# Splitting the late score products of a fused WKV and MoE kernel into high and low parts

## The chip, the cores and the metric

The kernel runs on one core of one Trainium2 chip. The metric is the device time of one execution in microseconds; lower is better. Before the change the median of three runs is 518.88 us (518.77 to 519.77).

## The reference

Two stages follow each other. The first is a linear attention with decay over `(batch 4, heads 8, time 768, head size 48)`:

```python
for t in range(S):
    cur = einsum('bhd,bhe->bhde', u[None] * k_t, v_t)
    y[:, :, t] = einsum('bhd,bhde->bhe', r_t, state + cur)
    state = w[None, :, :, None] * state + einsum('bhd,bhe->bhde', k_t, v_t)
```

The second takes `x`, which is `y` as 3072 tokens of 384 numbers, through two matrices with 2048 hidden columns. The inputs and the output are float32.

```python
h = x @ w_in          # 3072x384 @ 384x2048
g = h * cos(h)
out = g @ w_out       # 2048x384
```

## The kernel before

**Attention.** Time is cut into chunks of 128 steps; there are 24 chunks (`chunk(i, ...)`, batch `i % 4`). Inside a chunk the recurrence is turned into matrix products: the scores `A = k·r` of all pairs of time steps (`mm_a`, line 785), a mask (`mask`, L791) that keeps one triangle and leaves on the diagonal what ScalarE wrote there (`diagonal`, L775), the products of the scores with `v` and of the carried state with `r` (`mm_x` L805, `mm_x2` L818), and the update of the state (`mm_z` L840). Heads lie in pairs: head `2p` in partitions 0 to 47 and head `2p+1` in partitions 64 to 111, so `kT` and `rT` hold 4 pairs of 112 partitions x 128 columns, and a chunk has 4 x 2 score products. They are float32; the trace records each as two weight loads (PEld) and two products (PE), 16 of each for a chunk.

The first 12 chunks (`i < XS`) are transposed on TensorE (L696). The other 12 are called `late`: `k` and `r` come in by a second, staged load into the ring `raw` (L659), VectorE transposes them (L704) into `kT` and `rT`, and GpSimd multiplies them with the decay tables (L709). Then `mm_a` runs, and later `mm_xz` with the other products of the chunk.

**MoE.** The tokens form 8 blocks of three chunks (384 columns). Each matrix is kept as a high and a low float32r part, made while the kernel runs (`conv`), and so are `x` (`xh`, `xl`: rings of 12 chunk slots, `R_x`) and `g` (`gh`, `gl`). A product is the sum of three: high·high, high·low, low·high (`mm_h` L282, `mm_o` L288), each one load of 128x128 weights and one product with 384 columns. One step is one block with one group of 128 hidden columns: 9 products of L282, the chain on ScalarE and VectorE (`qi`, `rest`, `cos`, `gate`, `gh`, `gl`), and 9 products of L288. There are 128 steps. The first four blocks go through the hidden columns in turn in four cuts (steps 0 to 63), the other four one after the other.

**Order.** Every operation is an `op` with an engine, a planner's cost, a due time, what it comes after, and the buffers it holds. A list planner (`Plan.order`) gives each engine its order, once, when the program is built; at run time the engines only wait for data and buffers. Loads are issued from the SP queue; a buffer is free again when all its users have run. `xb` gives chunk `i` the slot `i % 12` of `x`'s ring.

**Clock-keeping.** Where the planner sees TensorE idle at the start, `warm_up(n)` puts in small bfloat16 products (L1050). `before` is true until the first `h` has been put out (`o_first`).

Of the kernel before, what the change touches and what calls it, by code (L numbers as in the profile page):

```python
# [15 lines left out]
ALU = mybir.AluOpType  # L16
# [16 lines left out]
XS = 12  # L33
# [40 lines left out]
class Plan:  # L74
# [9 lines left out]
    def op(self, eng, due, cost, emit, after=(), bufs=(), lat=0.2, line=None, port=False):  # L84

        o = Op(eng, due, cost, lat, emit, after, bufs, self.lines.get(line) if line else None, port)
        if line:
            self.lines[line] = o
        self.ops.append(o)
        return o  # L90
# [126 lines left out]
def kernel(  # L217
# [11 lines left out]
    nc = tc.nc  # L229
    PSUM = bass.MemoryType.PSUM  # L230

    B, H, S, D = r.shape
# [3 lines left out]
    C = 128  # L236
    NP = H // 2
    DP = 64
    KP = DP + D
# [3 lines left out]
    NJ = B * CPB  # L243
    TB = max(BLOCKS) * C
    NBLK = len(BLOCKS)
    FIRST = [sum(BLOCKS[:n]) for n in range(NBLK)]
# [22 lines left out]
    def f32(ap):  # L269
        return ap.bitcast(F32)  # L270


    def mm_h(ph, x_hi, x_lo, f):

        fs = slice(f * P, (f + 1) * P)
        mm = []
        for kk in range(NK):
            mm.append((w_in_hi[:, kk, fs], x_hi[:, :, kk, :]))
            mm.append((w_in_hi[:, kk, fs], x_lo[:, :, kk, :]))
            mm.append((w_in_lo[:, kk, fs], x_hi[:, :, kk, :]))  # L280
        for i, (a, b_) in enumerate(mm):
            nc.tensor.matmul(ph, a, b_, start=(i == 0), stop=(i == len(mm) - 1))  # L282
# [19 lines left out]
    with ExitStack() as actx:  # L302
# [19 lines left out]
        xh = att.tile([P, XS, NK, C], F32R, name="xh")  # L322
        xl = att.tile([P, XS, NK, C], F32R, name="xl")
        R_x = [Tile((xh[:, i], xl[:, i])) for i in range(XS)]
# [34 lines left out]
        op = plan.op  # L359
        PE, DVE, ACT, POOL, SP, ACTQ = "PE", "DVE", "ACT", "POOL", "SP", "ACTQ"  # L360
# [22 lines left out]
        def start_dve():  # L383
# [14 lines left out]
            lat=2.2,  # L398
# [41 lines left out]
        def tab_copy():  # L440
# [11 lines left out]
            lat=3.0,  # L452
# [5 lines left out]
        def flag_load():  # L458
            nc.sync.dma_start(b_wr()[0:1, :], w.rearrange("(o h) d -> o (h d)", o=1))
# [144 lines left out]

        last_A = [None]
        last_z = [None] * B

        def flat(buf, p):  # L610
# [8 lines left out]
        def cube(buf):  # L619
            return buf().rearrange("q (p t) -> q p t", p=NP)  # L620

        def chunk(i, due, xbuf):
# [8 lines left out]
            kT, rT = Buf(R_kT), Buf(R_rT)  # L631
            Ap = [Buf(bk) for _ in range(2)]
# [11 lines left out]

            late = i >= XS
            if late:
                rb = Buf(R_f)
                ks, rs = Buf(R_raw), Buf(R_raw)

# [50 lines left out]
            if late:  # L700
# [7 lines left out]
                def decay_s(dst, dec):  # L708
                    return lambda: nc.gpsimd.tensor_tensor(dst()[0:KP], dst()[0:KP], dec[0:KP], op=ALU.mult)  # L709

                t_k = op(DVE, due - 2.9, 0.95, tr_s(kT, ks), [l_ks], [ks, kT])
                e_k = op(POOL, due - 2.8, 1.4, decay_s(kT, decT_k), [t_k], [kT], port=True)
                t_r = op(DVE, due - 2.8, 0.95, tr_s(rT, rs), [l_rs], [rs, rT])
                e_r = op(POOL, due - 2.7, 1.4, decay_s(rT, decT_r), [t_r], [rT], port=True)
            else:
                t_r = op(PE, due - 2.4, 0.49, tr(rTp, rb), [l_r, o_pool], [rb, rTp, rT], lat=0.3)
                e_r = op(
                    DVE,
                    due - 2.2,
                    0.62,  # L720
                    lambda: nc.vector.tensor_tensor(rT()[0:KP], cube(rTp)[0:KP], decT_r[0:KP], op=ALU.mult),  # L721
                    [t_r, o_dtr],
                    [rTp, rT],
                )
# [16 lines left out]
            if first:  # L741
                t_k = op(PE, due - 2.5, 0.49, tr(kTp, kb), [l_k, o_pool], [kb, kTp, kT], lat=0.3)
                e_k = op(
                    DVE,
                    due - 2.3,
                    0.62,
                    lambda: nc.vector.tensor_tensor(kT()[0:KP], cube(kTp)[0:KP], decT_k[0:KP], op=ALU.mult),
                    [t_k, o_dtk],
                    [kTp, kT],
                )  # L750
# [3 lines left out]
            if not first and not late:  # L754
                t_k = op(PE, due - 2.5, 0.49, tr(kTp, kb), [o_kd, o_pool], [kb, kTp, kT], lat=0.3)
                e_k = op(ACT, due - 2.3, 0.5, lambda: nc.scalar.copy(kT()[0:KP], cube(kTp)[0:KP]), [t_k], [kTp, kT])  # L756
# [14 lines left out]
            def diagonal(j):  # L771
                def go():
                    for p in range(NP):
                        h = 2 * p + j
                        nc.scalar.activation(A[j]()[:, p, :], ident, AF.Copy, scale=ab()[:, h : h + 1])  # L775

                return go

            o_d = [op(ACT, due - 1.55 + 0.01 * j, 1.18, diagonal(j), [o_a, o_pool], [ab, A[j]], line="diagonal") for j in range(2)]

            def mm_a():
                for p in range(NP):
                    for j in range(2):
                        ps = slice(j * DP, j * DP + D)
                        nc.tensor.matmul(cube(Ap[j])[:, p, :], kT()[ps, p, :], rT()[ps, p, :], start=True, stop=True)  # L785

            last_A[0] = o_A = op(PE, due - 1.7, 1.25 if late else 1.1, mm_a, [e_k, e_r], [kT, rT, *Ap], lat=0.3)


            def mask(j):  # L790
# [45 lines left out]
            def mm_z():  # L836
                z = zp()[:, 0 : NP * D].rearrange("q (p e) -> q p e", p=NP)
                for h in range(H):
                    p, j = divmod(h, 2)
                    nc.tensor.matmul(z[j * DP : j * DP + D, p, :], kb()[:, h, 0:D], vb()[:, h, 0:D], start=True, stop=True)  # L840
# [10 lines left out]
            if late:  # L851
# [8 lines left out]
                    lat=0.3,  # L860
# [38 lines left out]
        first_h, last_h, need_f = {}, {}, {}  # L899
# [4 lines left out]
        block_of = [n for n in range(NBLK) for _ in range(BLOCKS[n])]  # L904


        xb = [Buf([R_x[i % XS]]) for i in range(NJ)]
        x_ready, x_ready_of = {}, {}
        for i in range(NJ):
            n = block_of[i]  # L910
            t = i - FIRST[n]
            if i < XS:
                due = -6 + 0.9 * i
            else:
                lo, hi = first_h[n - 1], first_h[n] - 1
                if i >= XS:
                    lo = max(lo, last_h[block_of[i - XS]])
                due = lo + (hi - lo) * (t + 1) / BLOCKS[n]
            x_ready.setdefault(n, []).extend(chunk(i, due, xb[i]))
            x_ready_of[i] = x_ready[n][-1]  # L920
# [4 lines left out]
        for i in range(2 * NF):  # L925
            f, part = divmod(i, 2)
            g = max(x for x in group if x <= f)
            if g == 0:
                due = 2 * i - 3.0
            else:  # L930
                lo = need_f[max(x for x in group if x < g)] + 1
                hi = need_f[g] - 1
                n_g = 2 * sum(1 for x in range(NF) if max(y for y in group if y <= x) == g)
                due = lo + (hi - lo) * (i - 2 * g + 1) / n_g
# [3 lines left out]
        lo = need_f[NF - 1] + 10  # L938
# [6 lines left out]
        for s, (n, f, f0, f1) in enumerate(steps):  # L945
# [3 lines left out]
            ph, q, qi, gh, gl = Buf(B_H if n >= GRP else B_HX), Buf(R_f), Buf(R_qi), Buf(R_gh), Buf(R_gl)  # L949
            xs = [xb[FIRST[n] + t] for t in range(nt)]  # L950

            def h(ph=ph, n=n, nt=nt, f=f):
                j = FIRST[n] % XS
                mm_h(ph()[:, 0 : nt * C], xh[:, j : j + nt], xl[:, j : j + nt], f)

            oh = op(PE, s, 9 * (0.0058 + 0.000437 * w_), h, [*x_ready[n], w_ready[2 * f]], [ph, *xs], lat=0.3, line="h")
            if s == 0:
                o_first = oh
            if s in look:
                checks.append(check_range(look[s], s + 4, oh))  # L960
            if s == NS - 14:
# [42 lines left out]
            for t in range(nt):  # L1004
# [6 lines left out]
                if f == f1 - 1:  # L1011
# [16 lines left out]
                    def st(ob=ob, dst=dst, f0=f0, last=last):  # L1028
# [14 lines left out]
                        lat=2.5,  # L1043
# [3 lines left out]
        def warm_up(n):  # L1047
            wp = B_WARM.ap[:, 0:256].rearrange("q (a b) -> q a b", a=2)
            for _ in range(n):
                nc.tensor.matmul(wp, warm, warm[:, None, :].to_broadcast([P, 2, P]), start=True, stop=True)  # L1050

        order = plan.order(PASSES)
        before = True
        with tc.manual_schedule():
            for o in order:
                if before and o.eng == PE:
                    n = int(min(o.gap, 6.0) / 0.2)
                    if n:
                        warm_up(n)
                    before = o is not o_first  # L1060
                o.emit()


# [2 lines left out]
    with tc.If(ok < 1):  # L1066
        with ExitStack() as gctx:
            cp = gctx.enter_context(tc.tile_pool(name="cp", bufs=1))
            for i in range(2 * NF):
                f, part = divmod(i, 2)  # L1070
# [4 lines left out]
                if part == 0:  # L1075
# [4 lines left out]
                    hi, lo, av = w_in_hi[:, :, fs], w_in_lo[:, :, fs], ca.rearrange("p (kk f) -> p kk f", kk=NK)  # L1080
                else:
                    nc.sync.dma_start(raw.rearrange("p f w -> p (f w)"), w_out_w[fs, :])
                    hi, lo, av = w_out_hi[:, f, :], w_out_lo[:, f, :], ca
# [62 lines left out]
            with tc.For_i(0, NT // P, 1) as it:  # L1146
# [10 lines left out]
                for f in range(NF):  # L1157
                    ph = gps.tile([P, P], F32, name="ph")
                    mm_h(ph, x_hi[:, None], x_lo[:, None], f)
                    q = gp.tile([P, P], F32, name="gq")  # L1160
# [41 lines left out]
```

## Time and profile before

| | before |
|---|---|
| median of the runs | 518.88 us |
| the profiled execution | 517.88 us, span 516.2 us |
| mean granted TensorE clock | 0.996 |
| PE busy | 505.9 us (98%) |
| PEld busy (weight loads, beside PE) | 481.3 us (93%) |
| VectorE (DVE) busy | 382.5 us (74%) |
| ScalarE (ACT) busy | 331.7 us (64%) |
| GpSimd (POOL) busy | 177.7 us (34%) |
| score products L785, 384 records | 27.9 us PE, 23.3 us PEld |

A row of a timeline reads: start in us from the span's start, length in us, engine, line, operation, `out<-in`, partitions x columns of weights and of the moving operand, how many records were merged, and in brackets how long the engine was idle before and what ended it. PE is the product, PEld the weight load that belongs to it. A group row gives busy us and mean ns of one.

### The profile page before, as it was taken

How to read it: one execution, taken by the hardware profiler on the slowest of the kernel's cores; microseconds unless marked ns; L12 is line 12 of the kernel's file. 1: busy time of each engine (PE TensorE's matmuls, PEld its weight loads, DVE VectorE, ACT ScalarE, POOL GpSimd, SP SyncE). 2: the span in 40 equal slices, each digit the busy share in tenths (PEclk: the TensorE clock that was granted, in tenths of full speed). 3: DMA queues.
4: the chain of work that ended last, by engine and by line, in shares of the span. 5: the costliest groups of instructions: out<-in, count | busy, mean ns of one | idle time of the engine just before them, and what ended most of it. 6: DMA issues, size and time to landing. Idle time of an engine off the chain costs nothing.

```text
span 516.2 us, 11762 instructions
## 1 busy us (share of the span) xinstructions
PE 505.9 (98%) x4401; PEld 481.3 (93%) x4401; DVE 382.5 (74%) x773; ACT 331.7 (64%) x833; POOL 177.7 (34%) x184
## 2 busy tenths in 40 slices
PE   8999999999999999999999999999999999999994
PEld 6778899999999999999999999999999999999993
DVE  6899889887887876666777777787776768656552
ACT  2979888777776656546667565575665764745452
POOL 6785622364444452242426134214044041300000
PEclk9999999999999999999999999999999999999998
DMA  8996345477775593424675736446265455200001
GB/s 139 182 190 142 76 140 181 141 138 164 159 154 114 138 187 53 65 75 54 161 155 144 161 98 167 111 161 151 83 150 141 144 153 134 67 35 14 1 1 53
DMA packets 114980, 61.61 MB, mean 119 GB/s; under 512 B 78433, under 2 KB 110818, under 8 KB 114914
## 3 DMA queue, kind: packets, MB, share of 16 engines
q1 hardware_dynamic: 109586, 53.50, 42.2%
q0 software_dynamic: 5184, 7.08, 9.8%
q8 instruction: 36, 0.59, 0.5%
q14 instruction: 30, 0.25, 0.2%
q10 hardware_dynamic: 144, 0.20, 0.1%
HBM read 48.96 MB, written 11.80 MB: 118 GB/s over the span
## 4 chain that ended last, share of the span: by engine, by line
PE 95%; DVE 1%; ACT 1%; issue 0%
PE bank L288 40%; PE bank L282 39%; PE bank L785 5%; PE bank L818 4%; PE bank L805 3%; PE bank L696 2%; PE bank L840 2%; PE bank L1050 1%; ACT A L775 0%; DVE A L791 0%; ACT zt L833 0%; DVE zc L887 0%; DVE rT L721 0%; ACT kT L756 0%; DVE w_in_lo L597 0%
## 5 line engine op out<-in xcount | busy, mean ns | idle before, releaser
L288 PE MATMUL bank<-w_out_hi,gh 128*128 128x384 f32 x384 | 132.0, 344 | 0.0
L282 PE MATMUL bank<-xh,w_in_lo 128*128 128x384 f32 x384 | 129.7, 338 | 0.5 <-DVE w_in_lo L597 0.5
L288 PE MATMUL bank<-w_out_hi,gl 128*128 128x384 f32 x384 | 129.7, 338 | 0.0
L288 PE MATMUL bank<-w_out_lo,gh 128*128 128x384 f32 x384 | 129.4, 337 | 0.0
L282 PE MATMUL bank<-xh,w_in_hi 128*128 128x384 f32 x384 | 129.1, 336 | 0.0
L282 PE MATMUL bank<-xl,w_in_hi 128*128 128x384 f32 x384 | 128.7, 335 | 0.0
L296 DVE SCALAR_TENSOR_TENSOR f<-bank,qi 128x384 f32<-128x384 f32 (+1 forms) x132 | 71.2, 542 | 44.3 <-ACT qi L293 43.4
L293 ACT ACTIVATE qi<-bank 128x384 int32<-128x384 f32 (+1 forms) x132 | 62.7, 478 | 55.3 <-PE bank L282 54.6
L989 ACT CAST gh<-f 128x384 fp32r<-128x384 f32 (+1 forms) x132 | 65.7, 500 | 48.6 <-DVE f L986 48.2
L986 DVE TENSOR_TENSOR f<-bank,f 128x384 f32<-128x384 f32 (+1 forms) x132 | 71.1, 541 | 34.8 <-ACT f L299 32.7
L299 ACT ACTIVATE f<-f 128x384 f32<-128x384 f32 (+1 forms) x132 | 67.4, 513 | 44.1 <-DVE f L296 43.3
L992 DVE TENSOR_TENSOR gl<-f,gh 128x384 fp32r<-128x384 f32 (+1 forms) x132 | 79.9, 608 | 19.4 <-ACT gh L989 18.6
L288 PEld LDWEIGHTS bank<-w_out_hi,gh 128*128 128x128 f32 x384 | 72.0, 187 | 3.2 <-issue 1.2
L282 PEld LDWEIGHTS bank<-xh,w_in_lo 128*128 128x128 f32 x384 | 72.1, 188 | 0.8 <-DVE w_in_lo L597 0.8
L282 PEld LDWEIGHTS bank<-xh,w_in_hi 128*128 128x128 f32 x384 | 72.1, 188 | 0.5 <-ACT A L775 0.2
L282 PEld LDWEIGHTS bank<-xl,w_in_hi 128*128 128x128 f32 x384 | 72.1, 188 | 0.0
L288 PEld LDWEIGHTS bank<-w_out_hi,gl 128*128 128x128 f32 x384 | 72.0, 188 | 0.0
L288 PEld LDWEIGHTS bank<-w_out_lo,gh 128*128 128x128 f32 x384 | 72.0, 187 | 0.0
L775 ACT ACTIVATE A<-ident,a 128x128 f32<-128x128 f32 x192 | 59.7, 390 | 6.0 <-DVE a L766 5.9
L709 POOL TENSOR_TENSOR kT<-kT,decT_k 112x512 f32<-112x512 f32 x12 | 15.6, 1301 | 127.6 <-PE bank L282 65.1
L587 POOL TENSOR_TENSOR f<-f,raw 128x384 int32<-128x384 int32 x32 | 36.4, 1137 | 65.9 <-DVE f L576 28.8
L1034 POOL DMA_DIRECT2D out_dram<-f x36 | 32.7, 1012 | 40.1 <-ACT f L1019 31.2
(88 smaller groups left out, 597.1 us busy)
## 6 DMA issues: line engine op xcount, KB each, us to landing
raw<-in_moe_w_in_dram SPq DMA_DIRECT2D x32, 384.0 KB, 3.4
raw<-in_moe_w_out_dram SPq DMA_DIRECT2D x32, 384.0 KB, 3.4
out_dram<-f POOLq DMA_DIRECT2D x36, 192.0 KB, 4.6
k<-in_k_dram SPq DMA_DIRECT2D x24, 192.0 KB, 3.5
v<-in_v_dram SPq DMA_DIRECT2D x24, 192.0 KB, 4.4
raw<-in_k_dram SPq DMA_DIRECT2D x47, 96.0 KB, 2.5
raw<-in_r_dram SPq DMA_DIRECT2D x47, 96.0 KB, 2.5
out_dram<-f SPq DMA_DIRECT2D x23, 192.0 KB, 2.0
```

The lines of the kernel that those rows point to most:

```text
L282: nc.tensor.matmul(ph, a, b_, start=(i == 0), stop=(i == len(mm) - 1))
L288: nc.tensor.matmul(acc, a[:, ts], b_[:, f, :], start=(first and i == 0), stop=(last and i == 2))
L293: nc.scalar.activation(qi, ph, AF.Copy, scale=INV_2PI, bias=0.25)
L296: nc.vector.scalar_tensor_tensor(q, ph, INV_2PI, qi, op0=ALU.mult, op1=ALU.subtract)
L299: nc.scalar.activation(q, q, AF.Sin, scale=TWO_PI, bias=0.5 * math.pi)
L587: lambda: nc.gpsimd.tensor_tensor(ai(), ai(), cn(), op=ALU.add),
L775: nc.scalar.activation(A[j]()[:, p, :], ident, AF.Copy, scale=ab()[:, h : h + 1])
L785: nc.tensor.matmul(cube(Ap[j])[:, p, :], kT()[ps, p, :], rT()[ps, p, :], start=True, stop=True)
L986: nc.vector.tensor_tensor(g()[:, cs], ph()[:, cs], q()[:, cs], op=ALU.mult)
L989: nc.scalar.copy(gh()[:, cs], g()[:, cs])
L992: nc.vector.tensor_tensor(gl()[:, cs], g()[:, cs], f32(gh())[:, cs], op=ALU.subtract)
L1034: nc.gpsimd.dma_start(dst, ob(), accum_op=ALU.add)
```

## The change

The scores of the 12 late chunks are made of three products of high and low parts, as `mm_h` does it. For `kT` and for `rT`, ScalarE copies the float32 values into a float32r part (the high one) and VectorE subtracts this from the values to give the low one. The four parts lie in slots 3, 4 and 5 of `x`'s ring (`xh` for high, `xl` for low), so no new memory is taken; a late chunk's `two` must find these three slots free. The planner's cost of late scores goes from 1.25 to 0.95. The late chunks' own `x` no longer uses slots 3 to 5: block 4 takes slots 0 to 2, block 5 slots 6 to 8, block 6 slots 9 to 11 and block 7 again 0 to 2. And `warm_up` ends at the first score products (`first_A[0]`) in place of the first `h`.

```diff
-        last_A = [None]
+        last_A, first_A = [None], []
...
+                two = [Buf([R_x[n]]) for n in (3, 4, 5)]
...
+            def part(n, low):
+                xs_ = (xl if low else xh)[:, 3:6].rearrange("q i kk t -> q (i kk t)")
+                return xs_[:, n * NP * C : (n + 1) * NP * C].rearrange("q (p t) -> q p t", p=NP)
+
             def mm_a():
+                if late:
+                    mm = ((part(0, 0), part(1, 0)), (part(0, 0), part(1, 1)), (part(0, 1), part(1, 0)))
+                else:
+                    mm = ((kT(), rT()),)
                 for p in range(NP):
-                    for j in range(2):
-                        ps = slice(j * DP, j * DP + D)
-                        nc.tensor.matmul(cube(Ap[j])[:, p, :], kT()[ps, p, :], rT()[ps, p, :], start=True, stop=True)
-
-            last_A[0] = o_A = op(PE, due - 1.7, 1.25 if late else 1.1, mm_a, [e_k, e_r], [kT, rT, *Ap], lat=0.3)
+                    for n, (a, b_) in enumerate(mm):
+                        for j in range(2):
+                            ps = slice(j * DP, j * DP + D)
+                            nc.tensor.matmul(
+                                cube(Ap[j])[:, p, :], a[ps, p, :], b_[ps, p, :], start=(n == 0), stop=(n == len(mm) - 1)
+                            )
+
+            a_in, a_bufs = [e_k, e_r], [kT, rT]
+            if late:
+
+                def split(n, src):
+                    return (
+                        lambda: nc.scalar.copy(part(n, 0)[0:KP], src()[0:KP]),
+                        lambda: nc.vector.tensor_tensor(
+                            part(n, 1)[0:KP], src()[0:KP], f32(part(n, 0))[0:KP], op=ALU.subtract
+                        ),
+                    )
+
+                a_in, a_bufs = [], two
+                for n, (src, made) in enumerate(((kT, e_k), (rT, e_r))):
+                    high, low = split(n, src)
+                    o_h = op(ACT, due - 2.5, 0.5, high, [made], [src, *two])
+                    a_in.append(op(DVE, due - 2.3, 0.62, low, [o_h], [src, *two]))
+            last_A[0] = o_A = op(PE, due - 1.7, 0.95 if late else 1.1, mm_a, a_in, [*a_bufs, *Ap], lat=0.3)
+            first_A.append(o_A)
...
-        xb = [Buf([R_x[i % XS]]) for i in range(NJ)]
+        slot = [i if i < XS else (0, 6, 9)[(i - XS) // 3 % 3] + i % 3 for i in range(NJ)]
+        xb = [Buf([R_x[i]]) for i in slot]
...
-                    lo = max(lo, last_h[block_of[i - XS]])
+                    lo = max(lo, last_h[block_of[max(n for n in range(i) if slot[n] == slot[i])]])
...
-                j = FIRST[n] % XS
+                j = slot[FIRST[n]]
...
-                    before = o is not o_first
+                    before = o is not first_A[0]
```

More of the change, by code (lines that the diff above doesn't have):

```diff
@@ L952, in h @@
             def h(ph=ph, n=n, nt=nt, f=f):
-                j = FIRST[n] % XS
+                j = slot[FIRST[n]]
                 mm_h(ph()[:, 0 : nt * C], xh[:, j : j + nt], xl[:, j : j + nt], f)
             oh = op(PE, s, 9 * (0.0058 + 0.000437 * w_), h, [*x_ready[n], w_ready[2 * f]], [ph, *xs], lat=0.3, line="h")
-            if s == 0:
-                o_first = oh
             if s in look:
```

## The prediction

> **What bounds the kernel now.** I read the page first, then the table of stretches, then the timeline of TensorE around one late chunk, then its weight loads.
>
> ```profile
> span 516.2 us, 11762 instructions
> ...
> PE 95%; DVE 1%; ACT 1%; issue 0%
> ...
> 230.00:280.00 50.00, 50.00 (x423) 48.24 (x422) 36.34 (x70) 32.00 (x83) 19.15 (x19) 1.00 0.56 123
> 280.00:330.00 50.00, 50.00 (x489) 47.36 (x489) 37.93 (x77) 31.53 (x84) 13.72 (x13) 1.00 0.60 140
> ```
>
> The chain that ended last is TensorE for 95% of the span. In the stretches that hold late chunks its busy time is the whole stretch (50.00 of 50 us) at a granted clock of 1.00, while VectorE has some 12 us free in 50 and ScalarE 18. So a microsecond more or less on TensorE there is a microsecond of the result, and work on the other two is covered as long as TensorE does not come to wait for it.
>
> ```profile
> 216.07 0.34 PE L288 MATMUL bank<-w_out_hi,gl 128*128 128x384 f32 x1
> 216.25 0.34 PE L288 MATMUL bank<-w_out_lo,gh 128*128 128x384 f32 x1
> 216.52 1.16 PE L785 MATMUL bank<-rT,kT 48*128 48x128 f32 x16
> 217.61 0.44 PE L288 MATMUL bank<-w_out_hi,gh 128*128 128x384 f32 x1
> 217.89 0.34 PE L288 MATMUL bank<-w_out_hi,gl 128*128 128x384 f32 x1
> ...
> 443.97 1.16 PE L785 MATMUL bank<-rT,kT 48*128 48x128 f32 x16
> ```
>
> These are the first late chunk's scores among MoE products (the last row is the twelfth's). MoE products start 0.18 apart (216.07 to 216.25). From 216.25 to 217.89 there are 1.64 us, of which two MoE products explain 0.35: the scores cost 1.29 us of TensorE in each late chunk. What sets that time is seen in the weight loads.
>
> ```profile
> 216.52 0.97 PEld L785 LDWEIGHTS bank<-rT,kT 48*128 48x128 f32 x16 [0.25 <-issue]
> 217.61 0.19 PEld L288 LDWEIGHTS bank<-w_out_hi,gh 128*128 128x128 f32 x1
> 217.72 0.19 PEld L288 LDWEIGHTS bank<-w_out_hi,gl 128*128 128x128 f32 x1
> 217.89 0.19 PEld L288 LDWEIGHTS bank<-w_out_lo,gh 128*128 128x128 f32 x1
> ...
> 216.52 0.19 PEld L785 LDWEIGHTS bank<-rT,kT 48*128 48x128 f32 x2 [0.25 <-issue]
> ...
> 220.95 0.14 PEld L805 LDWEIGHTS bank<-rT,zt 112*32 112x32 f32 x5 [0.25 <-issue]
> ```
>
> The sixteen loads go two at a time (two within one 0.19: the head pair's two row groups side by side), so there are 8 pairs in 0.97 us. Less the last load's 0.19 this is 7 steps: 0.112 us from pair to pair. The loads of L288 show that this is what 128 columns of weights take: the load at 217.61 finds TensorE empty after the scores, and the next follows at 217.72, 0.11 later, before the first 384-column product has gone through; only the third (217.89) waits for a product. With 32 columns (L805) the fifth load starts 0.14 less one load's 0.11, so 0.03, after the first four.
>
> ```profile
> L785 PEld LDWEIGHTS bank<-rT,kT 48*128 48x128 f32 x384 | 23.3, 187 | 5.8 <-issue 3.2 <-ACT kT L756 1.4 <-ACT A L775 0.6
> L282 PEld LDWEIGHTS bank<-xl,w_in_hi 128*128 128x128 f32 x384 | 72.1, 188 | 0.0
> L282 PEld LDWEIGHTS bank<-xh,w_in_hi 128*128 128x128 f32 x384 | 72.1, 188 | 0.5 <-ACT A L775 0.2 <-issue 0.2
> L805 PEld LDWEIGHTS bank<-rT,zt 112*32 112x32 f32 x480 | 11.9, 109 | 4.3 <-issue 3.2 <-DVE f L986 0.2 <-DVE f L296 0.2
> ```
>
> A load of 128 float32r columns (L282, 188 ns) is as long as one of 128 float32 columns (L785, 187 ns); from 32 to 128 columns it grows by 78 ns (187 less 109), 0.82 ns a column, so 128 columns hold the load path for 0.105 us. The same weights used by two products in a row (`w_in_hi` with `xh`, then `xl`) are loaded twice: 384 loads each.
>
> **The score products.** Before, a late chunk has 8 float32 products in 16 records: 8 pairs. After, it has 4 x 3 x 2 = 24 float32r products of one record each: 12 pairs, with the high part of `k` loaded twice. What a pair takes no row shows directly: no float32r product here is narrower than 384 columns. From below: the MoE products' 0.174 us for 384 columns, scaled to 128, gives 0.058. From above: if single-pass products of two row groups did not run side by side, 2 x 0.112. I take 0.112, the row nearest to it in every respect (same line, same 128 columns of weights, same 48 rows), since the load of the next weights can't go faster than 0.105 to 0.112 however short the product is. So four more pairs, 4 x 0.112 = 0.45, less about 0.05 because the last product of the block, with one pass of 0.058 in place of 0.112, ends sooner: **+0.40 us a chunk, +4.8 us for 12** (0.35 to 0.45: 4.2 to 5.4). The turns into and out of the 48-row shape (0.25 idle for "issue" in the row above) stay as many and are taken as unchanged.
>
> **The splits.** Each late chunk adds two copies on ScalarE and two subtractions on VectorE.
>
> ```profile
> L756 ACT COPY kT<-bank 112x512 f32<-112x512 f32 x10 | 5.7, 574 | 2.2 <-PE bank L696 2.2
> L992 DVE TENSOR_TENSOR gl<-f,gh 128x384 fp32r<-128x384 f32 x126 | 78.4, 623 | 19.4 <-ACT gh L989 18.6
> L597 DVE TENSOR_TENSOR w_in_lo<-f,w_in_hi 128x384 fp32r<-128x384 f32 x16 | 9.2, 572 | 0.4
> ```
>
> The copy has the shape of L756: 2 x 0.57. The subtraction is that of L597 with 512 columns in place of 384: 0.57 x 512/384 = 0.76, twice. That is 1.15 us of ScalarE and 1.5 us of VectorE a chunk. A chunk passes every 20.7 us (216.52 to 443.97 in 11 steps), so VectorE goes from 37 to some 41 of 50 us: covered, cost 0. The chain to the scores grows by 0.57 + 0.76 plus two handovers. If the cover went (splits always the last thing that scores wait for), up to 1.3 us a chunk.
>
> **The slots.** The parts need slots 3 to 5, which block 1 reads up to step 51.
>
> ```profile
> 0.00:225.00 225.00, 89.42 (x467) 1.00 0.66 136
> ```
>
> Filtered to L282, there are 467 products up to 225.00; 52 steps are 468. So block 1 is done with its slots at about 225.3, and the first late chunk's scores, now at 216.52, can't start before 225.3 + 0.57 + 0.76, about 227. TensorE has MoE steps 52 to 63 to do meanwhile, which need no late chunk, and two more late chunks have until 270 (step 64): 43 us for three. Cost 0; if the written order let TensorE wait, once up to 1.6 us. The copies queue on ScalarE ahead of later `qi`, `cos` and `gh`; an early place would hold these, and with them L288. The later slots (6 to 8, 9 to 11, 0 to 2) are free long before their chunks. No DMA is added; SP and POOL get nothing new, though the staged loads move with the scores, whose `raw` buffers are still freed by VectorE's transposes.
>
> **The warm-up.** Twelve of the 43 warm-up products come after the first scores.
>
> ```profile
> L1050 PE MATMUL bank<-warm 128*128 128x256 bf16 x43 | 8.9, 343 | 1.1 <-DVE pq L385 1.1
> ...
> 11.69 0.28 PE L1050 MATMUL bank<-warm 128*128 128x256 bf16 x1
> 15.83 0.28 PE L1050 MATMUL bank<-warm 128*128 128x256 bf16 x1
> 16.38 0.27 PE L1050 MATMUL bank<-warm 128*128 128x256 bf16 x1
> 16.93 0.71 PE L1050 MATMUL bank<-warm 128*128 128x256 bf16 x5
> 21.88 0.27 PE L1050 MATMUL bank<-warm 128*128 128x256 bf16 x1
> 28.57 0.28 PE L1050 MATMUL bank<-warm 128*128 128x256 bf16 x1
> 29.72 0.39 PE L1050 MATMUL bank<-warm 128*128 128x256 bf16 x2
> 33.78 0.44 PE L282 MATMUL bank<-xh,w_in_lo 128*128 128x384 f32 x1 [0.45 <-DVE w_in_lo L597]
> ...
> 0.00:32.00 32.00, 30.00 (x426) 23.40 (x428) 25.32 (x54) 19.80 (x57) 23.91 (x39) 1.00 1.07 160
> ...
> 480.00:517.00 37.00, 28.63 (x164) 28.31 (x162) 15.32 (x39) 14.73 (x39) 0.00 (x0) 0.93 0.06 19
> ```
>
> Five take 0.71 less one product's 0.27 in four steps: 0.11 each, so 12 are 1.3 us. What is late next is the conversion of the weights: at 33.78 TensorE already waits 0.45 us for `w_in_lo`, which no warm-up delays. So most of it turns into waiting; I take -0.2 us. Bounds: -1.3 if nothing waits; and, since the granted clock is 1.00 in the first 32 us but 0.93 in the last 37, where TensorE has gaps, +1.6 if gaps took it to 0.93 from 10.6 to 33 us (7% of 22).
>
> **The new order.** Other planner costs give another order in all places. After 80 us TensorE has nothing to gain (no idle time), so I take 0, with ±1.
>
> **The sum.** +4.8 - 0.2 = +4.6 us: span 520.8. The profiled execution took 517.88 us, 1.68 more than its span, so it would be 522.5; the median is 1.00 above that execution, so I forecast **523.5 us**. Its own range: 4.2 - 1.3 - 1 to 5.4 + 1.6 + 1 are the extremes; most of it lies in 522 to 526.
>
> **The rivals.**
> - *Short products run at their streaming time (faster).* If a 128-column weight load hid fully, a pair would take 0.058: 12 x 0.058 = 0.70 against 8 x 0.112 = 0.90, -0.20 a chunk, -2.4, with the warm-up -2.6: 516.3 us. It decides below a pair time of 0.079 (12 x 0.079 = 0.90 + 0.05). For it speaks that a MoE product of three times the columns takes only 0.174; against it the 0.11 between the loads at 217.61 and 217.72. Chance 0.14. The Trainium skill, "TensorE: Matmul & The Clock Gate", section "Back-to-back issue gap", gives N/2.4 + 2.5 ns for a warm product, 56 ns at 128 columns; by that estimate it would be -2.7 for the scores, but the page itself says that this leaves weight loads out.
> - *Loads partly hidden (same).* If pairs settled between the two, at 0.08, a chunk would gain or lose under 0.09 us: about +0.4 - 0.2, 519.1 us. Nothing in this trace shows such spacing for 128 columns of 32-bit weights. Chance 0.07. That section gives 81 ns a product at 128 columns for a stream of loads and products, by which estimate the scores would be at +0.3 us in all; the loads in rows above, 105 to 112 ns for 128 columns, speak against taking it over here.
> - *No side by side (much slower).* At 0.224 a pair, 24 x 0.112 = 2.69 against 0.90: +1.79 a chunk, +21: 540 us. For it: no row shows float32r in two row groups; against: float32 does it in every pair. Chance 0.06.
> - *The splits come late (slower).* TensorE waits up to 1.3 us more in each chunk: 523.5 + 15.6, 539 us. For it: two more handovers between in-order engines; against: no wait of TensorE after 80 us and 20.7 us for each chunk. Chance 0.05.
>
> **How the numbers follow.** The forecast has 0.68. What can't be told from no change is 0.2%, 1.04 us. Faster is the first rival less what its upper edge loses: 0.13. Same is the second and that edge: 0.07. Slower is the rest: 0.80. The two dear rivals (0.11) stay outside the range; it reaches down to 516.0 to take in the second and most of the first, and up to 526.
>
> **What would show it.** Right: L785 with 12 x 24 late records, a late block of loads of about 1.4 us (11 x 0.112 + 0.19) against 0.97, and between the MoE products around it 1.7 us against 1.29; TensorE still without waits after 80 us; first late scores after 225; 31 warm-up products. Wrong: a late block of loads under 1.1 us (first rival), loads one by one (third), or L785 waiting for the subtraction (fourth); a granted clock below 1.00 before 33 us would break the warm-up term.

## The result, and the profile after

| | before | after |
|---|---|---|
| median of three runs | 518.88 us | 525.25 us (524.44 to 525.98) |
| ratio | | 1.0126, 95% interval 1.0109 to 1.0143 |
| the profiled execution | 517.88 us, span 516.2 | 525.98 us, span 524.3 |
| records of late scores on PE | 192 | 288 |
| DVE busy | 382.5 us | 404.0 us |

The change made the kernel 1.26% slower, 6.5 us by the ratio and 6.4 by the medians. The forecast was 523.5 us in a range of 516.0 to 526.0. In the changed kernel the score products are line 797, the high copy 806, the subtraction 807, the gate 1016, `gl` 1022, the GpSimd lines 710, 732, 740 and 761, and the warm-up 1080.

The page of the changed kernel, span and chain; then its table of stretches (columns as in the table of before: PE, PEld, DVE, ACT, POOL busy us):

```profile
span 524.3 us, 11992 instructions
...
PE 89%; ACT 2%; DVE 1%; DMA 1%; issue 1%; POOL 1%; ACTq 0%; POOLq 0%
...
280.00:330.00 50.00, 49.93 (x447) 47.64 (x446) 41.12 (x82) 35.41 (x93) 18.76 (x17) 1.00 0.60 143
330.00:380.00 50.00, 49.53 (x488) 47.04 (x486) 40.84 (x78) 31.43 (x83) 13.30 (x11) 1.00 0.52 132
```

TensorE still sets the time, but no longer alone: its share of the chain went from 95 to 89%, and in two stretches that it filled to 50.00 before it now misses 0.07 and 0.47 us. Its first late score block, in the timeline of PE and then of the loads:

```profile
225.05 0.34 PE L282 MATMUL bank<-xh,w_in_lo 128*128 128x384 f32 x1
225.31 0.33 PE L797 MATMUL bank<-xh 48*128 48x128 f32 x2
225.48 0.27 PE L797 MATMUL bank<-xl,xh 48*128 48x128 f32 x2
...
226.59 0.28 PE L797 MATMUL bank<-xh,xl 48*128 48x128 f32 x2
226.80 0.44 PE L288 MATMUL bank<-w_out_hi,gh 128*128 128x384 f32 x1
227.08 0.34 PE L288 MATMUL bank<-w_out_hi,gl 128*128 128x384 f32 x1
```

```profile
225.31 0.19 PEld L797 LDWEIGHTS bank<-xh 48*128 48x128 f32 x2 [0.25 <-ACT f L299]
225.42 0.19 PEld L797 LDWEIGHTS bank<-xl,xh 48*128 48x128 f32 x2
...
226.54 0.19 PEld L797 LDWEIGHTS bank<-xh,xl 48*128 48x128 f32 x2
```

Twelve pairs of loads from 225.31 to 226.54: 11 steps of 0.112 us. From the block's start to the next MoE product there are 226.80 - 225.31 = 1.49 us, against 217.61 - 216.52 = 1.09 before. On the mean of the twelve blocks it is 1.485 against 1.092: +0.39 in each.

Where the profiled execution's 8.1 us are (steps found by counting L282's products in nines): 4.7 in the twelve score blocks; 0.4 at the start (step 46's first product at 204.8 against 204.4); 1.8 between steps 46 and 127, all of it between one MoE product and the next, in waits that were not there before; 1.2 from the last step's first product to the end (16.3 against 15.1 us). The last part is scatter: over the profiles of this study it ranged from 13.5 (e6 below) to 16.3, with 16.2 in e9, whose late scores are float32 as before. The profiled execution was the slowest of the three.

What can hold VectorE, and what TensorE then waits for, is seen in groups of the changed kernel (mean ns is the number before the last bar), and in one collision in the timelines of DVE and POOL:

```profile
L806 ACT CAST xh<-kT 112x512 fp32r<-112x512 f32 x12 | 7.4, 619 | 1.2 <-POOL kT L710 0.5 <-PE bank L282 0.2
L807 DVE TENSOR_TENSOR xl<-kT,xh 112x512 fp32r<-112x512 f32 x12 | 16.7, 1391 | 1.4 <-ACT xh L806 1.2
L807 DVE TENSOR_TENSOR xl<-rT,xh 112x512 fp32r<-112x512 f32 x12 | 13.8, 1146 | 4.1 <-ACT xh L806 4.0
...
336.41 2.32 DVE L807 TENSOR_TENSOR xl<-kT,xh 112x512 fp32r<-112x512 f32 x1
...
335.91 1.29 POOL L710 TENSOR_TENSOR rT<-rT,decT_r 112x512 f32<-112x512 f32 x1 [0.28 <-DVE rT L705]
337.17 1.02 POOL L761 TENSOR_TENSOR f<-f,u_b 128x384 f32<-128x384 f32 x1
338.14 1.48 POOL L740 TENSOR_TENSOR k<-k,dec_k 128x384 f32<-128x384 f32 x1
```

The subtractions take 0.67 to 3.50 us for the same shape, 30.4 us in all where 24 of the shortest would be 16. The one at 336.41 began while GpSimd worked, went on through the next GpSimd instruction, and ended at 338.73, 0.54 after that one's end. All that VectorE had queued was late by this, the gate (L1016) first. The longest of TensorE's new waits came four microseconds later (PE, DVE, ACT):

```profile
342.67 0.34 PE L288 MATMUL bank<-w_out_lo,gh 128*128 128x384 f32 x1
343.48 0.45 PE L282 MATMUL bank<-xh,w_in_hi 128*128 128x384 f32 x1 [0.47 <-DVE f L1016]
...
342.87 0.56 DVE L1016 TENSOR_TENSOR f<-bank,f 128x384 f32<-128x384 f32 x1 [0.47 <-ACT f L299]
...
339.29 0.52 ACT L1019 CAST gh<-f 128x384 fp32r<-128x384 f32 x1 [2.40 <-DVE f L1016]
...
341.15 1.27 ACT L776 ACTIVATE A<-ident,a 128x128 f32<-128x128 f32 x4
342.33 0.51 ACT L299 ACTIVATE f<-f 128x384 f32<-128x384 f32 x1
```

TensorE starts `h` 0.81 after the product before it, where 0.17 is usual; it waits for a bank that the gate reads, the gate for the cosine, the cosine for ScalarE's diagonal. ScalarE had stood idle for 2.40 us until the gate behind the long subtraction let it go on at 339.29, and from there to the cosine at 342.33 it had no pause: the chain that ended last runs from the subtraction at 336.41 over the gate and ScalarE to `h` at 343.48. Shorter waits follow the products at 275.6 (0.17 beyond the usual), 282.5 (0.24) and 427.4 (0.24), and after each of the four the next product comes 0.27 to 0.28 later in place of 0.17.

A long subtraction need not cost anything. The longest one, 3.50 us at 261.22, has no wait of TensorE in the 14 us after its start; and in the kernel before `gl` takes up to 1.88 us beside GpSimd's work, where 0.55 is usual, without any wait between MoE products.

### The profile page after: what moved, and what is told of

The parts are those of the page before. It is cut to its first block, busy times and chain, and to the rows that moved or that the text cites. A ratio compares the mean times of both kernels' runs of the same rounds, so it can differ in the third digit from the quotient of the medians.

```text
span 524.3 us, 11992 instructions
## 1 busy us (share of the span) xinstructions
PE 510.5 (97%) x4485; PEld 485.4 (93%) x4485; DVE 404.0 (77%) x797; ACT 344.0 (66%) x857; POOL 181.7 (35%) x184
## 4 chain that ended last, share of the span: by engine, by line
PE 89%; ACT 2%; DVE 1%; DMA 1%; issue 1%; POOL 1%; ACTq 0%; POOLq 0%
PE bank L288 38%; PE bank L282 37%; PE bank L797 5%; PE bank L849 3%; PE bank L836 3%; PE bank L871 1%; PE bank L697 1%; DMA k<-in_k_dram 1%; ACT A L776 1%; DVE xl L807 1%; DVE f L1016 0%; POOL f L732 0%; ACT kT L757 0%; ACT zt L864 0%; ACT qi L293 0%
## 5 line engine op out<-in xcount | busy, mean ns | idle before, releaser
L282 PE MATMUL bank<-xh,w_in_hi 128*128 128x384 f32 x384 | 129.5, 337 | 0.6 <-DVE f L1016 0.5
L282 PE MATMUL bank<-xh,w_in_lo 128*128 128x384 f32 x384 | 129.6, 337 | 0.0
L282 PE MATMUL bank<-xl,w_in_hi 128*128 128x384 f32 x384 | 128.9, 336 | 0.0
L1016 DVE TENSOR_TENSOR f<-bank,f 128x384 f32<-128x384 f32 (+1 forms) x132 | 71.2, 542 | 31.6 <-ACT f L299 29.7
L1022 DVE TENSOR_TENSOR gl<-f,gh 128x384 fp32r<-128x384 f32 (+1 forms) x132 | 74.2, 566 | 22.6 <-ACT gh L1019 21.8
L282 PEld LDWEIGHTS bank<-xh,w_in_hi 128*128 128x128 f32 x384 | 72.1, 188 | 2.3 <-DVE f L1016 1.7
L282 PEld LDWEIGHTS bank<-xl,w_in_hi 128*128 128x128 f32 x384 | 72.1, 188 | 0.3 <-DVE xl L904 0.3
L282 PEld LDWEIGHTS bank<-xh,w_in_lo 128*128 128x128 f32 x384 | 72.2, 188 | 0.1
```

The source lines that it names most:

```text
L1016: nc.vector.tensor_tensor(g()[:, cs], ph()[:, cs], q()[:, cs], op=ALU.mult)
L1022: nc.vector.tensor_tensor(gl()[:, cs], g()[:, cs], f32(gh())[:, cs], op=ALU.subtract)
```

## The experiments

Each kernel was compared with the kernel before on the same chip. "Products" is what its twelve late score blocks take beyond those of the kernel before, and "waits" what lies between its MoE products beyond the kernel before, from step 46 to step 127; both are in us and from the one profiled execution (changed kernel: +4.7 and 1.8).

| run | edit to | us | ratio and interval | products | waits |
|---|---|---|---|---|---|
| e1_two_products | after | 520.30 | 1.0048 (1.0026 to 1.0071) | -0.6 | 2.5 |
| e2_half_moving | after | 524.21 | one run | +4.5 | 1.7 |
| e3_half_weights | after | 518.90 | one run | -2.6 | 3.6 |
| e4_warm_kept | after | 525.68 | 1.0143 (1.0122 to 1.0165) | +4.7 | 2.1 |
| e5_f32_scores | after | 520.70 | 1.0042 (1.0026 to 1.0058) | 0 | 2.4 |
| e6_port | after | 525.19 | 1.0117 (1.0086 to 1.0147) | +4.8 | 5.1 |
| e7_warm_only | before | 518.37 | 0.9987 (0.9974 to 1.0000) | 0 | 0.0 |
| e8_port_price | e6 | 523.64 | 1.0095 (1.0078 to 1.0112) | +4.7 | 0.5 |
| e9_slots_only | after | 519.04 | 1.0004 (0.9995 to 1.0014) | 0 | 0.0 |
| e10_f32_port_price | e8 | 521.43 | 1.0056 (1.0033 to 1.0079) | 0 | 2.1 |
| e11_wide | after | 526.95 | one run | +6.9 | 1.6 |
| e12_sub_on_pool | e8 | 524.29 | 1.0116 (1.0096 to 1.0136) | +4.7 | 1.2 |

### What sets the time of a product pair

```diff
# e2_half_moving (late)
-  nc.tensor.matmul(cube(Ap[j])[:, p, :], a[ps, p, :], b_[ps, p, :], ...)
+  nc.tensor.matmul(cube(Ap[j])[:, p, 0:64], a[ps, p, :], b_[ps, p, 0:64], ...)
# e3_half_weights (late)
+  nc.tensor.matmul(cube(Ap[j])[0:64, p, :], a[ps, p, 0:64], b_[ps, p, :], ...)
# e11_wide (late): pp = slice(p // 2 * 2, p // 2 * 2 + 2)
+  nc.tensor.matmul(cube(Ap[j])[:, pp, :], a[ps, p, :], b_[ps, pp, :], ...)
```

> Late score products move 64 columns of r in place of 128 (half of the scores are left out); weights stay 128 columns. Theory (weight loads set the pair time): pairs stay 0.112 us apart, late blocks 1.45 to 1.49 us, time within 0.5 us of the changed kernel. Rival (the product's streaming sets it): pairs about 0.06 apart, late blocks about 0.8 us, about 8 us less.

> Late score products load 64 columns of k in place of 128 (half of the scores are left out); r stays 128 columns wide. Theory (weight loads set the pair time): loads take half, the pairs go to 0.058 us (the product's own time for 128 columns, from 0.174 for 384), late blocks about 0.85 us, about 7.5 us less than the changed kernel. Rival (the product, or a fixed cost of each, sets it): pairs stay at 0.112, no change.

> Each late score product moves 256 columns (two head pairs' worth of r, so the scores are left wrong) with 128 columns of weights as in the changed kernel; 12 pairs. Theory (the load of 0.112 us hides a product of up to about 256 columns, 0.174 x 256/384 = 0.116): pairs 0.112 to 0.120 apart, late blocks 1.45 to 1.6 us, time within 1 us of the changed kernel though twice the columns are moved. Rival (load and product partly add): pairs 0.17 or more, blocks over 2 us, 7 us more.

The loads of the first late block with 64 columns moved (e2), with 64 columns of weights (e3), and with 256 columns moved (e11); the score line is 798 in all three:

```profile
224.87 0.18 PEld L798 LDWEIGHTS bank<-xh 48*128 48x128 f32 x2 [0.25 <-ACT f L299]
224.98 0.19 PEld L798 LDWEIGHTS bank<-xl,xh 48*128 48x128 f32 x2
...
226.10 0.19 PEld L798 LDWEIGHTS bank<-xh,xl 48*128 48x128 f32 x2
```

```profile
224.29 0.13 PEld L798 LDWEIGHTS bank<-xh 48*64 48x64 f32 x2 [0.25 <-ACT f L299]
224.35 0.14 PEld L798 LDWEIGHTS bank<-xl,xh 48*64 48x64 f32 x2
...
224.95 0.14 PEld L798 LDWEIGHTS bank<-xh,xl 48*64 48x64 f32 x2
```

```profile
224.88 0.19 PEld L798 LDWEIGHTS bank<-xl,xh 48*128 48x128 f32 x2
225.00 0.19 PEld L798 LDWEIGHTS bank<-xh,xl 48*128 48x128 f32 x2
...
226.07 0.19 PEld L798 LDWEIGHTS bank<-xh,xl 48*128 48x128 f32 x2
```

Half the columns moved: (226.10 - 224.87)/11 = 0.112, unchanged. Half the weights: (224.95 - 224.29)/11 = 0.060. Twice the columns moved: (226.07 - 224.88)/10 = 0.119, little more. (e2's one run is 1.0 us under the changed kernel's median and 0.2 under its fastest run, where at most 0.5 was expected; e11's is 1.7 over the median, where at most 1 was, and its blocks make 2.2 of that, most of them 1.63 long.) So the load of the weights sets the pair's time, and a product of up to some 256 columns hides under it; for the pair times the theory held in all three. In e3 the product's own time, 0.058 by an estimate from 0.174 for 384 columns, lies as near to 0.060 as half a load does, so that run doesn't tell which of the two sets it. The times follow with a remainder: e3's blocks are 0.62 us shorter than the changed kernel's, 7.4 us in all, and its time is 6.4 us shorter; its trace has more waits of TensorE before `h` (one of 1.14 from product to product at 339.44, where 0.17 is usual). The Trainium skill, "TensorE: Matmul & The Clock Gate", section "LDWEIGHTS (loading the stationary operand)", gives columns/1.2 ns whatever the rows, by which an estimate is 107 ns for 128 columns and 53 for 64. The trace agrees to 5 ns for 128 columns, with 48 rows and two row groups side by side; e3's 0.060 is 7 ns above the figure for 64 and can't test it, as just said.

### How much of the loss the products are

```diff
# e1_two_products
-  mm = ((part(0, 0), part(1, 0)), (part(0, 0), part(1, 1)), (part(0, 1), part(1, 0)))
+  mm = ((part(0, 0), part(1, 0)), (part(0, 1), part(1, 0)))
# e5_f32_scores: mm = ((kT(), rT()),) for late chunks too
-  a_in, a_bufs = [], two
+  a_in, a_bufs = [], [kT, rT, *two]
```

> Leaves out the third product (low part of r) of each late score; order of all engines as in the changed kernel. Theory (the score block alone is on the path, 0.112 us for each pair of row groups): 8 pairs in place of 12, each late block 0.45 us shorter, 12 x 0.45 = 5.4 us less than the changed kernel's 525.25: about 519.9 us, still 1 us over the kernel before (518.88) although its blocks are then as short as before, the rest being what the splits and the start cost. Rival (TensorE waits for the splits, so shorter blocks turn into waiting): less than half of that comes back, 522.5 us or more.

> The changed kernel with the splits made and waited for, in the same order of all engines, but the late scores taken from kT and rT in float32 as before (8 pairs of records). Theory (scores are 4.75 us of the 6.4, the other 1.7 are splits, slots, order and the start): late blocks 1.09 us again, 520.5 us, 1.6 over the kernel before. Rival (splits and slots are free, all else was the start and the scatter of the runs): within 0.5 us of the kernel before.

Both leave the order of the other engines as in the changed kernel. The float32 scores' blocks are 1.09 us again, and the kernel stands 0.42% above the one before, 2.2 us, against 6.5: the products are worth 4.4 by these ratios and 4.7 by the blocks. The rival falls: what remains is clear of the kernel before. With two products the blocks are 1.04 us, 0.05 under those of before, and yet 2.5 us are left, 1.5 more than expected: part of the shorter blocks became waiting (0.80 for the low part of `x` at block 4's start, 0.81 from product to product at 339.94).

### The rest: warm-up, slots, splits

```diff
# e7_warm_only, to the kernel before
-  before = o is not o_first
+  before = o is not first_A[0]
# e4_warm_kept, to the kernel after: the reverse
# e9_slots_only: no split operations, float32 scores, price 1.25; two held as before
-  a_in, a_bufs = [], two
+  a_in, a_bufs = [e_k, e_r], [kT, rT, *two]
```

> The kernel before with only the end of the warm-up moved to the first scores. Theory (it makes no measurable difference): within 0.5 us of the kernel before, granted clock 1.00 in the first 32 us. Rival (it costs the start 0.5 us, as step 8 came 0.5 us later in the changed kernel): 0.5 us or more slower. Other rival (removed products are removed time): up to 1.3 us faster.

> The changed kernel with warm-up products up to the first h again (43 in place of 31); order otherwise the same. Theory (warm-ups after the first scores stand where TensorE waits anyway): within 0.3 us of the changed kernel, 525.0 to 525.6. Rival (the start lost 0.5 us, 85.0 against 84.5 us at step 8, because the warm-ups are gone): 0.5 us less, 524.7. Other rival (they were in the way): up to 1 us more.

> The changed kernel without the splits: late scores in float32 from kT and rT, priced 1.25, but still placed behind the freeing of slots 3 to 5, with the new slots and the early end of the warm-up. Theory (the splits' load on ScalarE and VectorE makes the 2 us that float32 scores with splits cost over the kernel before): those 2 us go, 518.2 us, 0.4 under the kernel before as with the warm-up's end alone. Rival (the later start of the first late chunks makes them, block 4 waiting for its third chunk): 520 us or more, with a wait of TensorE for x's low part near 273 us.

Ending the warm-up early gains 0.7 us on the kernel before (0 to 1.3 by the interval), and putting it back costs the changed kernel 0.9 by the ratios, with intervals that overlap. Both point the same way, but the size isn't settled. The rival that it cost the start 0.5 us falls: step 8 began at 85.0 in the changed kernel and 84.5 before, but at 83.9 in e7 and in e8, which end the warm-up early as well. Without splits the slots cost nothing that can be measured (0.2 us, -0.3 to 0.7). So the splits carry the rest: e5 against e9, 1.0042 against 1.0004, is 2.0 us. These two differ in the planner's price as well (0.95 and 1.25); e10 below has e9's price and differs from it by the splits alone, and there it is 2.7 us (1.0056 against 1.0004). The traces say the same: e7 and e9 have no wait between MoE products that the kernel before hasn't, and every kernel with splits has some.

### Why the splits cost anything

```diff
# e6_port
-  a_in.append(op(DVE, due - 2.3, 0.62, low, [o_h], [src, *two]))
+  a_in.append(op(DVE, due - 2.3, 0.68, low, [o_h], [src, *two], port=True))
# e8_port_price = e6 and
-  op(PE, due - 1.7, 0.95 if late else 1.1, mm_a, ...)
+  op(PE, due - 1.7, 1.65 if late else 1.1, mm_a, ...)
# e10_f32_port_price = e5 and the port, price 1.25
# e12_sub_on_pool = e8 and low on GpSimd, op(POOL, due - 2.3, 1.4, low, ..., port=True)
```

> The changed kernel with the subtraction declared to the planner as one that must not run beside GpSimd's work (port=True, cost 0.68). Theory (subtractions that run beside GpSimd take up to 3.5 us in place of 0.68, hold VectorE, and let TensorE wait some 1.3 us in all after 80 us): the longest subtraction falls to about 0.85 us, the waits of TensorE for the gate after 270 us go, 1 us less than the changed kernel: 524.2. Rival (ScalarE's crowding makes the waits, or the gain is lost to another order): subtractions short, time within 0.4 us of 525.3 or above.

> The kernel of the run with the port, and the late scores priced for the planner at 1.65, near what they take, in place of 0.95. Theory (the price only places other work, TensorE's work is the sum): within 0.5 us of the run with the port alone. Rival (the wrong price let the other engines' work bunch and made the waits): 1 us less than the run with the port.

> Float32 late scores with the splits made and waited for, the subtraction planned away from GpSimd's work (port=True, 0.68) and the scores priced 1.25. Theory (splits cost nothing once the order keeps them off GpSimd and off each other; the products are the whole loss): 4.75 us under the run with port and price, 518.9 us, within 0.3 of the kernel before. Rival (splits cost by their mere load): 520.5 us as with float32 scores in the old order.

> The run with port and price, with the two subtractions of each late chunk made on GpSimd in place of VectorE (planned at 1.4 us each). Theory (what the change costs beyond its products are waits that start with subtractions standing behind GpSimd's work on VectorE): no late subtraction holds VectorE, no wait of TensorE over 0.3 us after 80 us, about as the run with port and price: 523.0 to 523.9, that is the products' 4.75 us over the kernel before with little more. Rival (the longer GpSimd chain makes the third chunk of block 4 late): a wait near 273 us of 1 us or more, 524.5 us or above.

With the port (e6) the subtractions are shorter, 24.0 us in all against 30.4, the longest 2.40, not the 0.85 expected; the wait at 342 is gone, and another is there that is longer (PE, DVE, POOL of e6):

```profile
288.26 0.69 PE L282 MATMUL bank<-xh,w_in_hi 128*128 128x384 f32 x1 [3.06 <-DVE f L1016]
288.75 0.52 PE L282 MATMUL bank<-xl,w_in_hi 128*128 128x384 f32 x1
289.07 0.52 PE L282 MATMUL bank<-xh,w_in_lo 128*128 128x384 f32 x1
...
283.15 4.59 DVE L1022 TENSOR_TENSOR gl<-f,gh 128x384 fp32r<-128x384 f32 x1
...
282.91 1.58 POOL L710 TENSOR_TENSOR rT<-rT,decT_r 112x512 f32<-112x512 f32 x1
284.16 1.28 POOL L761 TENSOR_TENSOR f<-f,u_b 128x384 f32<-128x384 f32 x1
...
285.74 1.58 POOL L740 TENSOR_TENSOR k<-k,dec_k 128x384 f32<-128x384 f32 x1
```

It is the same collision with another subtraction: `gl`, 0.55 us alone, starts beside GpSimd's work and ends at 287.74, 0.42 after the third GpSimd instruction; the gate stands behind it, and TensorE is idle for 3.06 us. That wait costs more than its length: behind it the granted clock is 0.50 (288.20 to 291.40), the products up to 291.31 start 0.32 apart where 0.17 is usual, and some 1.5 us more are lost (an estimate: 0.31 at the first step and 0.15 at each of eight). So the gain was eaten by another order, as the rival had it. With the honest price as well (e8) the waits are nearly gone, in TensorE's list of waits:

```profile
PE bank L282 <- DVE xl L904: 0.3, 1, 0.3
```

and the time falls to 4.9 us over the kernel before, which is the products' 4.7 and almost nothing else. The gain on e6 is 1.1 us by the ratios, near the rival's 1, but the two intervals overlap. Yet e10, planned in the same manner with float32 scores, did not come to the kernel before's time: 1.0056, 2.9 us over it by the ratio and 2.3 by the medians, in executions from 520.1 to 525.4. Its longest wait is where block 4 starts, for the low part of its third chunk (the first row below). The longest of e12, which has no late subtraction on VectorE, is 5.6 us later, for the gate (the second):

```profile
275.74 0.45 PE L282 MATMUL bank<-xl,w_in_hi 128*128 128x384 f32 x1 [1.47 <-DVE xl L904]
```

```profile
281.30 0.45 PE L282 MATMUL bank<-xh,w_in_hi 128*128 128x384 f32 x1 [1.05 <-DVE f L1016]
```

What stands ahead of these two waits differs. In e10 the low part (L904, 275.14) stands on VectorE behind a transposition for the next late chunk (L705, 272.50), a gate and two updates of the state, of which one (L918) takes 0.95 beside GpSimd's work where 0.36 is usual. In e12 the gate stands behind a transposition of 1.08 us (L705, 279.78), and no collision is in the chain.

The theory of the collision is shown as a mechanism (the rows at 336.41 and 283.15) and fails as the whole account: moving the subtractions to GpSimd gave 1.0116, no better than the changed kernel, between what was expected of the theory and of the rival. Over the products, all else (with the warm-up's early end in it) costs 1.8 us in the changed kernel, 2.2 and 2.9 with float32 scores, 1.3 on GpSimd and 0.2 in e8. The same added work costs from almost nothing to 2.9 us, so it is not its mere load that costs. The planner's order differs between these kernels, but no run here isolates it. What makes one order good is open; not tried was a planner that knows of the collision on both sides. No version here beats the kernel before clearly; e7 comes nearest.

## Why the prediction was right, point by point

The direction, the mechanism of the main term and its size were right. That the time also lay in the range, 0.75 us below its upper end, was in part luck: the missing 1.8 us of the splits' term were covered by margins that had been set for the warm-up and the new order.

- **The score products**: right in mechanism and size. 0.112 us a pair was forecast and measured, and +4.7 us for +4.8. What decided it were two load rows 0.11 apart behind a score block, read as the time that 128 columns of weights take; e2 and e11 show that this reading was the right one: with half and with twice the columns moved the pairs stay 0.112 and 0.119 apart. The rival of short products at 0.058 a pair had a price that e3 comes near (0.060, with half the weights), but its condition, a hidden load, did not hold here at 128 columns. The loads go two at a time, as in float32, so the rival of products one by one fell too.
- **The loads' block**: 1.42 us (1.23 from first to last start and 0.19) where about 1.4 was forecast; the span between the MoE products around it is 227.08 - 225.05 = 2.03 with two products in it, so 1.68 where 1.7 was forecast.
- **The splits, "covered, cost 0"**: the step that failed. The term measured 1.8 us in the profiled execution, in waits of MoE products. The copies took 0.62 for 0.57; the subtractions took 1.39 and 1.15 on the mean for 0.76, since the size was scaled from a row (L597) whose operation is planned away from GpSimd's. (Alone they take 0.68. The row shown next to it, `gl` with 623 ns on the mean where 0.55 us is usual, had the collision in it.) The share of free time on VectorE (12 us in 50) was read as cover; but three engines in order hand the chain on, and one instruction of 2.3 us is late for all of them. "TensorE still without waits after 80 us" was wrong. The fourth rival had the place roughly (splits in the way of TensorE) but not the way: scores did not wait for the subtraction, `h` did, and at few chunks. The Trainium skill speaks against this step, and it was not weighed: "SBUF — State Buffer", section "Who interferes with whom", has it that a VectorE instruction with two SBUF inputs contends with a GpSimd instruction that reads SBUF, and the second to issue blocks until the first is done. The rows at 336.41 and 283.15 agree, and go further: the VectorE instruction waited through two and three GpSimd instructions in a row (by the recorded spans, which are rough on GpSimd).
- **The slots, cost 0**: right without splits (e9, 1.0004). With splits, the 43 us for the three chunks of block 4 were not always enough: where its first step starts, TensorE waits for the third chunk's low part, 1.6 us beyond the usual in e10, 1.0 in e1, 0.8 in e5, 0.5 in e8 and 0.2 in the changed kernel. The earliest start was off: 227 was forecast, 225.31 measured, because step 51 itself came 3.2 us earlier (220.5 for 223.8) once the first late chunk's products no longer stood before it.
- **The warm-up, -0.2**: the sign is right, the size was too small if anything (-0.7 in e7); it lies within its bounds, and the clock stayed at 1.00 in the first 32 us.
- **The new order, 0 with ±1**: +0.4 at the start in the profiled execution. Its three waits for `r`, 1.0 us, are for a transfer; such waits ranged from 0.2 to 1.8 us over the profiles.

## What to carry to other kernels

Count a small matrix product by its weight loads first: three cheaper passes are slower than two dear ones where each pass needs its own load of 128 columns and the moving side is narrower than about 256, as here. Read the price from two loads that follow each other with nothing in front of them. And a free third of an engine covers added work only if no single added instruction can be held up: look at what runs on GpSimd beside a VectorE instruction with both inputs in SBUF.

## What the runs showed of the hardware

- Weight loads of 32-bit values with their products: pairs in two row groups 0.112 us apart for 128 columns of weights, the same for 64 and 128 columns moved, 0.119 for 256; and 0.060 for 64 columns of weights with 128 moved.
- A subtraction of two SBUF operands on VectorE beside GpSimd's work was not let in between GpSimd instructions that followed closely: 2.32 us through two of them in place of 0.68, and 4.59 through three in place of 0.55. In all 14 traces together 283 of 2088 such subtractions (`gl` and those of the late chunks) took more than 0.60 or 0.72 us, and each of these overlapped a GpSimd instruction.
- After TensorE had stood idle for 3.06 us in e6, its granted clock was 0.50 for 3.2 us, and products of 384 columns started 0.32 us apart in place of 0.17. After the shorter waits of the changed kernel the clock stayed at 1.00 (343.40 to 346.00, behind 0.47 us).
